# Half-size products of an attention and feed-forward kernel: transposes moved right behind the scores, both lumps of products at the tile's end, results taken out one tile later

## The chip, the core and the metric

The kernel runs on one core of a Trainium2 chip. The metric is the device time of one execution in microseconds (us). The engines are named as in the profile: PE (TensorE matmul) with its weight loads PEld, DVE (VectorE), ACT (ScalarE), POOL (GpSimd), and SP, which issues the DMAs here.

## The reference

The first half is attention with a threshold: of each row of scores only those within `tau` of the row's maximum count. The second half is two matrix products with an activation between them.

```python
scores = scale * np.matmul(q, k.transpose(0, 1, 3, 2))        # 8 batches, 8 heads, 576 x 64
thresh = np.max(scores, axis=-1, keepdims=True) - tau
scores = np.where(scores >= thresh, scores, -1000000000.0)
attn = np.exp(scores - np.max(scores, axis=-1, keepdims=True))
attn = attn / (np.sum(attn, axis=-1, keepdims=True) + 1e-09)
x = np.matmul(attn, v)                                        # then to (4608, 512)
h = x @ w_in                                                  # 512 -> 2048
g = h * np.tanh(np.log1p(np.exp(np.minimum(h, 20.0))))        # h itself above 20
out = g @ w_out                                               # 2048 -> 512
```

## The kernel before

**Attention** runs over 32 head pairs (8 batches of four), each in nine tiles of 128 rows, so `NT` is 288. One pass of the loop at line 764 is the step `g`; `g % 9` is called the position of its tile here. The instructions of each engine keep the order in which the code issues them (class `InOrder`, line 60), so the order of calls in a step is the order on the engines. All their rows carry line 70, that of the helper; they are told apart by tile names.

In step `g`, PE makes the scores `s` of tile `g + 1` (`begin`), four matmuls, or eight for the tile of position 8. DVE takes the row maximum of tile `g` and two small scalings (`st`), ACT makes the exponential `e`, and DVE masks and sums it into `p` (`masked`). In the next step POOL scales `p` (`normalise`). In the step after that PE transposes it into PSUM (`transposes`): four blocks into `tp`, and in odd tiles and position 8 a fifth into `t` (`t5` in the code). One step later ACT copies them to `hi`, `lo` and `tk` (`evacuate`). Twice in a pair, in the steps of positions 8 and 4, PE multiplies them with the values into `y` (`values`), ten matmuls; ACT takes `y` out into `x` in the following step. `y` and `t` share one PSUM bank.

**The first product** `h = x @ w_in` is fed into the same loop, as a generator `stream` from which `advance(stream, n)` takes `n` matmuls. For batches 2 to 5 (`SEVEN`), in steps 117 to 260 (`FROM` to `TO`, in the code `seven`), `gemm1_seven` works with seven half-size products where eight would be needed. For each of eight `j` it makes the products named in `steps` (line 681), each of six matmuls of 288 columns. They use three accumulators `a`, `b`, `c` in PSUM that take turns in two banks (`psh`, tag `ph`), so a product needs the bank of the last but one before it, and that one's result has to be taken out first. A result leaves PSUM in one of two ways: ACT copies it to `hst` (`copy`; for two of the four copies POOL then adds the first result, from the list `sides`), or DVE adds it to what is in `hst` (`add`; the last one also issues the store of `hst` to DRAM and, a step later, the load of the weight sums `wt` three `j` ahead).

A tile has two products, except at positions 4 and 8, where `y` is made (`EVEN` is 0 there): seven tiles with fourteen products a pair, two `j`. The first product of a tile (a lump of six matmuls) stands right behind the scores, the transposes behind it, the second lump at the end of the step. When a product ends, the generator puts the taking out of its result into the list `leaves`. Those of the second lump are carried over to the next step (`waiting`): copies in front of the exponential, adds behind the reciprocal. Those of the first lump are issued in the same step, behind the exponential. At positions 0 and 5 `evacuate` stands behind the exponential, otherwise in front of everything that ACT does in the step.

Behind these come, in each step, the gathering of `y` (`done`), and the `chores`: splitting `q`, `k` and `x` into a high and a low part (a cast on ACT, a subtraction on POOL: `q`, `k`, `xh`, `xl`), and at the end of a batch the differences of `x` (subtractions on DVE, `parts_x`, and their splits, `parts_t`).

Of the kernel before, what the change touches and what calls it, by code (L numbers as in the profile page):

```python
# [135 lines left out]
def attention_moe(tc, q, k, v, tau, w_in, w_out, out):  # L136
# [3 lines left out]
    with ExitStack() as outer:  # L140
# [108 lines left out]
        with ExitStack() as first:  # L249
# [6 lines left out]
            with ExitStack() as att:  # L256
# [369 lines left out]
                def gemm1_seven(b, made):  # L626
# [27 lines left out]
                    def run(j):  # L654
# [17 lines left out]
                        def add(name, other, last=False):  # L672
# [9 lines left out]
                            ("a", "A", "b11", 0, nc.scalar, copy, "21"),  # L682
                            ("b", "1", "t2", 0, nc.scalar, copy, "12", True),
                            ("a", "B", "b21", 1, nc.scalar, copy, "11"),
                            ("b", "2", "t3", 0, nc.scalar, copy, "22", True),
                            ("c", "0", "t1", 0, nc.vector, add, "22", "22"),
                            ("b", "C", "t4", 1, nc.vector, add, "21", "21"),
                            ("c", "3", "b22", 1, nc.vector, add, "12", "12", True),
                        )
                        for bank, w, x, end, engine, kind, *names in steps:  # L690
                            for h in product(j, bank, w, x, end):
                                if h is not None:
                                    leaves.append((engine is nc.scalar, lambda h=h, kind=kind, names=names: kind(*names)(h)))
                                yield
# [43 lines left out]
                def leave_tile(g):  # L738
                    evacuate(g % 9, *tiles[g]["tp"], pairs[g // 9]["pt"])
                    del tiles[g]  # L740
# [23 lines left out]
                for g in range(NT + 6):  # L764
# [16 lines left out]
                    if seven and EVEN[g % 9]:  # L781
                        advance(stream, 6)
# [4 lines left out]
                    if 3 <= g < NT + 3:  # L787
                        if not (seven and g % 9 in (0, 5)):
                            leave_tile(g - 3)
                    for scalar, work in waiting:  # L790
                        if scalar:
                            work()
                    if ahead:
                        tiles[g - 2]["tp"] = transposes(g - 2)
                    done = ready
                    ready = []
                    for _ in range(5 if g >= SOON else PIECES):
                        if pieces:
                            work, then = pieces.pop(0)
                            work()  # L800
                            if then:
                                (done if g >= NT else ready).append(then)
# [6 lines left out]
                    if seven and g % 9 in (0, 5):  # L809
                        leave_tile(g - 3)  # L810
# [8 lines left out]
                    for scalar, work in [m for m in waiting if not m[0]] + leaves:  # L819
                        work()  # L820
                    leaves.clear()
                    while sides:
                        sides.pop(0)()
                    for gather, closed in done:
                        gather()
                        if closed is not None:
                            close_pair(g, closed)
                    for work in chores.pop(g, []):
                        work()
# [31 lines left out]
                    if not seven:  # L861
                        advance(stream, DRAIN if g >= NT else (SLOW if 78 <= g < FROM else EVEN)[g % 9])
                    if g < len(WARM[1]):
                        warm_up(WARM[1][g])
                    if not ahead and 2 <= g < NT + 2:
                        tiles[g - 2]["tp"] = transposes(g - 2)
                    if seven and EVEN[g % 9]:
                        advance(stream, 6)
# [185 lines left out]
```

## Time and profile before

| | us |
|---|---|
| three runs | 1356.60, 1356.62, 1355.78 |
| median | 1356.6 |
| the profiled execution, its own time | 1356.75 |
| its span | 1355.0 |
| stretch with half-size products (first to last matmul that reads `wt`) | 365 to 829 |

| busy, whole span | us | share |
|---|---|---|
| PE | 1295.1 | 96% |
| weight loads | 1144.3 | 84% |
| DVE | 953.6 | 70% |
| ACT | 864.3 | 64% |
| POOL | 828.4 | 61% |

A row of the profile's timeline has the start in us from the span's start, the duration, the engine, the line, the operation with output and inputs, and a count of merged instructions; in brackets how long the engine had been idle and what ended that. Matmuls are pipelined: the step from one start to the next tells what one costs, and their durations overlap. A row of the waits has the engine and tile that waited, what for, the total in us, the count and the longest.

### The profile page before, as it was taken

Reading aid. Unit: us, or ns where it says so; the run is one execution under the profiler, and the core shown is the slowest. Engines: PE = TensorE matmul, PEld = TensorE weight load, DVE = VectorE, ACT = ScalarE, POOL = GpSimd, SP = SyncE. Lnnn points to the kernel's source line nnn. Section 1 sums busy time; section 2 is a strip of 40 time slices with the busy share of each in tenths; the row PEclk is TensorE's granted clock in tenths of the full one; section 3 lists DMA queues with packets and bytes.
Section 4 is the critical chain, followed back from the end, with each engine's and each line's share of the span. In section 5 each row is a group of like instructions: output and inputs, shape, how many; then the busy total and the mean of one; then the engine's idle time right before and its main releaser. Section 6 shows DMA issues by size and latency. Waiting matters only on the chain. (4 is left out here: it accounts for less than half of the span.)

```text
span 1355.0 us, 28749 instructions
## 1 busy us (share of the span) xinstructions
PE 1295.1 (96%) x9749; PEld 1144.3 (84%) x9749; DVE 953.6 (70%) x2564; ACT 864.3 (64%) x1716; POOL 828.4 (61%) x1165
## 2 busy tenths in 40 slices
PE   8787999999999999999999999999999999999998
PEld 5445899898878878877887888989979999999998
DVE  6998887777766766676676666563986666666664
ACT  4786887777766666676666666664656555555552
POOL 3788897777876786787678677642403334444331
PEclk9987999999999999999999999999999999999999
DMA  5444455767456546545645655313745443444440
GB/s 175 119 128 129 142 163 149 221 201 228 142 173 195 153 151 186 166 148 179 189 152 158 188 161 170 99 42 100 249 150 156 125 140 110 140 141 137 138 131 32
DMA packets 174434, 205.17 MB, mean 151 GB/s; under 512 B 29392, under 2 KB 147152, under 8 KB 170192
## 3 DMA queue, kind: packets, MB, share of 16 engines
q1 hardware_dynamic: 174288, 203.34, 49.5%
q8 instruction: 77, 1.26, 0.4%
q14 instruction: 69, 0.57, 0.1%
HBM read 143.52 MB, written 59.77 MB: 150 GB/s over the span
## 5 line engine op out<-in xcount | busy, mean ns | idle before, releaser
L70 DVE SCALAR_TENSOR_TENSOR p<-s,st,e 128x576 f32<-128x576 f32 x288 | 234.8, 815 | 204.6 <-ACT e L70 204.3
L70 POOL TENSOR_SCALAR p<-p,st 128x576 f32<-128x576 f32 x288 | 246.1, 854 | 92.9 <-DVE st L70 37.5
L70 ACT ACTIVATE e<-s,st 128x576 f32<-128x576 f32 x288 | 216.3, 751 | 133.1 <-DVE st L70 129.2
L70 PE MATMUL s<-k,q 128*128 128x288 f32 (+1 forms) x1280 | 237.7, 331 | 31.0 <-DVE p L70 28.5
L70 POOL TENSOR_TENSOR z<-z 128x256 f32<-128x256 f32 x128 | 124.4, 976 | 223.0 <-DVE z L70 214.2
L70 PEld LDWEIGHTS s<-k,q 128*128 128x128 f32 (+1 forms) x1280 | 172.5, 190 | 57.0 <-DVE p L70 51.8
L70 DVE TENSOR_REDUCE st<-s 128x1 f32<-128x576 f32 x288 | 216.7, 753 | 2.7 <-PE s L70 2.7
L70 DVE TENSOR_TENSOR gl<-z,gh 128x1792 fp32r<-128x1792 f32 (+1 forms) x72 | 141.7, 1969 | 108.1 <-ACT gh L70 108.1
L70 PE MATMUL h<-xh,w1h 128*128 128x288 f32 x704 | 212.4, 302 | 2.6 <-DVE hst L70 2.0
L70 ACT CAST gh<-z 128x1792 fp32r<-128x1792 f32 (+1 forms) x72 | 116.6, 1621 | 149.7 <-issue 81.1
L70 PE MATMUL h<-xl,w1h 128*128 128x288 f32 x704 | 208.9, 297 | 0.7 <-POOL xl L70 0.7
L70 PE MATMUL h<-xh,w1l 128*128 128x288 f32 x704 | 208.1, 296 | 0.0
L70 PE MATMUL tp<-ident,p 128*128 128x128 f32 x1152 | 179.8, 279 | 4.5 <-POOL p L70 2.8
L70 PEld LDWEIGHTS tp<-ident,p 128*128 128x128 f32 x1152 | 134.3, 141 | 45.1 <-issue 16.4
L70 PE MATMUL o<-gh,sl 128*128 128x256 f32 x512 | 144.5, 282 | 0.0
L70 PE MATMUL o<-gl,sh 128*128 128x256 f32 x512 | 143.8, 281 | 0.0
L70 PE MATMUL o<-gh,sh 128*128 128x256 f32 x512 | 143.5, 280 | 0.0
L70 PE MATMUL y<-hi,vf 128*64 128x320 f32 (+1 forms) x512 | 141.4, 417 | 0.4 <-ACT tk L70 0.4
L70 PE MATMUL y<-lo,vf 128*64 128x320 f32 (+1 forms) x512 | 141.4, 417 | 0.0
L70 PEld LDWEIGHTS h<-xh,w1h 128*128 128x128 f32 x704 | 133.9, 190 | 4.5 <-DVE hst L70 2.9
L70 PE MATMUL o<-gl,w2h 128*128 128x256 f32 (+1 forms) x448 | 133.3, 298 | 1.3 <-DVE gl L70 1.3
L70 PE MATMUL o<-gh,w2h 128*128 128x256 f32 (+1 forms) x448 | 133.3, 298 | 1.3 <-DVE hst L70 1.3
(77 smaller groups left out, 3209.5 us busy)
## 6 DMA issues: line engine op xcount, KB each, us to landing
z<-hd SPq DMA_DIRECT2D x144, 256.0 KB, 3.1
wt<-sw SPq DMA_DIRECT2D x32, 1024.0 KB, 6.3
r<-q SPq DMA_DIRECT2D x112, 160.0 KB, 2.5
r<-k SPq DMA_DIRECT2D x112, 160.0 KB, 2.3
hd<-hst SPq DMA_DIRECT2D x56, 256.0 KB, 6.2
vf<-v SPq DMA_DIRECT2D x64, 160.0 KB, 3.8
out_t<-c SPq DMA_DIRECT2D x36, 256.0 KB, 2.4
dec<-w_in SPq DMA_DIRECT2D x32, 256.0 KB, 3.7
```

The source lines that it names most:

```text
L70: made = method(*args, **kwargs)
```

## The change

Only the stretch of batches 2 to 5 is touched. The transposes of a tile move up to stand right behind the scores, and the matmuls of `y` stand behind them. Both lumps are taken from the stream at the step's end, twelve matmuls in one go. All results are carried over to the next step, where copies and adds are issued behind the exponential, `normalise` and the gathering of `y`, in the order of the products. `evacuate` stands in front of the exponential in all positions. The core of the diff (left out: the engine's name goes from the rows of `steps`; `multiply` is the old loop over `pieces` under a name):

```diff
-                        for bank, w, x, end, engine, kind, *names in steps:
+                        for bank, w, x, end, kind, *names in steps:
...
-                                    leaves.append((engine is nc.scalar, lambda h=h, kind=kind, names=names: kind(*names)(h)))
+                                    leaves.append(lambda h=h, kind=kind, names=names: kind(*names)(h))
...
                     waiting, leaves[:] = leaves[:], []
-                    if seven and EVEN[g % 9]:
-                        advance(stream, 6)
...
                     if 3 <= g < NT + 3:
-                        if not (seven and g % 9 in (0, 5)):
-                            leave_tile(g - 3)
-                    for scalar, work in waiting:
-                        if scalar:
-                            work()
+                        evacuate((g - 3) % 9, *tiles[g - 3]["tp"], pairs[(g - 3) // 9]["pt"])
+                        del tiles[g - 3]
...
-                    for _ in range(5 if g >= SOON else PIECES):
-                        if pieces:
-                            work, then = pieces.pop(0)
-                            work()
-                            if then:
-                                (done if g >= NT else ready).append(then)
+                    if not seven:
+                        multiply(5 if g >= SOON else PIECES)
...
                         exponential(tiles[g]["s"], tiles[g]["st"], tiles[g]["e"])
-                    if seven and g % 9 in (0, 5):
-                        leave_tile(g - 3)
...
-                    for scalar, work in [m for m in waiting if not m[0]] + leaves:
-                        work()
-                    leaves.clear()
-                    while sides:
-                        sides.pop(0)()
                     for gather, closed in done:
                         gather()
                         if closed is not None:
                             close_pair(g, closed)
+                    for work in waiting:
+                        work()
+                    for work in sides:
+                        work()
+                    sides.clear()
+                    if seven:
+                        tiles[g - 2]["tp"] = transposes(g - 2)
+                        multiply(5)
...
-                    if not seven:
+                    if seven:
+                        advance(stream, 12 if EVEN[g % 9] else 0)
+                    else:
                         advance(stream, DRAIN if g >= NT else (SLOW if 78 <= g < FROM else EVEN)[g % 9])
...
-                    if not ahead and 2 <= g < NT + 2:
+                    if not ahead and not seven and 2 <= g < NT + 2:
                         tiles[g - 2]["tp"] = transposes(g - 2)
-                    if seven and EVEN[g % 9]:
-                        advance(stream, 6)
```

PE, the tile of position 3 in the first pair of the stretch, before (`tp` and `t_` are the transposes, `h` the products, those from `w1h` and `w1l` being the first product of the next `j`):

```order
L70 MATMUL s<-k_4902,q_4901 128x288
L70 MATMUL s<-k_4903,q_4901 128x288
L70 MATMUL h<-xh,wt 128x288
L70 MATMUL h<-xl,wt 128x288
L70 MATMUL h<-xh,wt 128x288 x2
L70 MATMUL h<-xl,wt 128x288
L70 MATMUL h<-xh,wt 128x288
L70 MATMUL tp<-ident,p 128x128 x4
L70 MATMUL t_5618<-ident,p 128x128
L70 MATMUL h<-xh,w1h 128x288
L70 MATMUL h<-xl,w1h 128x288
L70 MATMUL h<-xh,w1l 128x288
```

And the same place of the change:

```order
L70 MATMUL s<-k_4902,q_4901 128x288
L70 MATMUL s<-k_4903,q_4901 128x288
L70 MATMUL tp<-ident,p 128x128 x4
L70 MATMUL t_5600<-ident,p 128x128
L70 MATMUL h<-xh,wt 128x288
L70 MATMUL h<-xl,wt 128x288
L70 MATMUL h<-xh,wt 128x288 x2
L70 MATMUL h<-xl,wt 128x288
L70 MATMUL h<-xh,wt 128x288
L70 MATMUL h<-xh,w1h 128x288
L70 MATMUL h<-xl,w1h 128x288
L70 MATMUL h<-xh,w1l 128x288
```

The five transposes changed places with the first lump of six.

ACT, positions 0 and 1 of a pair, before (`h_7592` and `h_7631` are the two banks of the products, `tp_` and `t5_` the transposes, `y_7551` the values' result):

```order
L70 ACTIVATE e_7600<-s_7546,st_7599 128x576
L70 COPY hi1_7503<-tp_7582 128x4x128
L70 COPY hst_7609<-h_7592 128x288
L70 COPY x_7611<-y_7551 128x256
L70 CAST q0_7520<-r_7527 128x320
L70 CAST q0_7520<-r_7529 128x320
L70 COPY tk1_7505<-t5_7629 128x128
L70 COPY lo1_7504<-tp_7624 128x4x128
L70 COPY hst_7609<-h_7631 128x288
L70 ACTIVATE e_7653<-s_7587,st_7652 128x576
L70 COPY hst_7609<-h_7592 128x288
L70 CAST q1_7523<-r_7577 128x320
```

And of the change:

```order
L70 COPY hi1_7495<-tp_7567 128x4x128
L70 ACTIVATE e_7594<-s_7545,st_7593 128x576
L70 COPY x_7602<-y_7550 128x256
L70 CAST q0_7520<-r_7527 128x320
L70 CAST q0_7520<-r_7529 128x320
L70 COPY tk1_7497<-t5_7609 128x128
L70 COPY lo1_7496<-tp_7604 128x4x128
L70 ACTIVATE e_7644<-s_7587,st_7643 128x576
L70 COPY hst_7652<-h_7622 128x288
L70 COPY hst_7652<-h_7629 128x288
L70 CAST q1_7523<-r_7582 128x320
```

The copy of `tp` stands in front of the first exponential instead of behind it, `x` right behind it, and both product copies stand behind the second exponential.

More of the change, by code (lines that the diff above doesn't have):

```diff
@@ L681, in run @@
                         steps = (
[L682 to L688, printed above, removed]
+                            ("a", "A", "b11", 0, copy, "21"),
+                            ("b", "1", "t2", 0, copy, "12", True),
+                            ("a", "B", "b21", 1, copy, "11"),
+                            ("b", "2", "t3", 0, copy, "22", True),
+                            ("c", "0", "t1", 0, add, "22", "22"),
+                            ("b", "C", "t4", 1, add, "21", "21"),
+                            ("c", "3", "b22", 1, add, "12", "12", True),
                         )
-                        for bank, w, x, end, engine, kind, *names in steps:
+                        for bank, w, x, end, kind, *names in steps:
                             for h in product(j, bank, w, x, end):
                                 if h is not None:
-                                    leaves.append((engine is nc.scalar, lambda h=h, kind=kind, names=names: kind(*names)(h)))
+                                    leaves.append(lambda h=h, kind=kind, names=names: kind(*names)(h))
                                 yield
@@ L736, in product, with multiply @@
                         pieces.append((some[-1], (gather, pi if t == 8 else None)))
-                def leave_tile(g):
-                    evacuate(g % 9, *tiles[g]["tp"], pairs[g // 9]["pt"])
-                    del tiles[g]
+                def multiply(n):
+                    for _ in range(n):
+                        if pieces:
+                            work, then = pieces.pop(0)
+                            work()
+                            if then:
+                                ready.append(then)
                 def close_pair(g, pi):
@@ L787, in attention_moe @@
                     if 3 <= g < NT + 3:
-                        if not (seven and g % 9 in (0, 5)):
-                            leave_tile(g - 3)
-                    for scalar, work in waiting:
-                        if scalar:
-                            work()
+                        evacuate((g - 3) % 9, *tiles[g - 3]["tp"], pairs[(g - 3) // 9]["pt"])
+                        del tiles[g - 3]
                     if ahead:
                         tiles[g - 2]["tp"] = transposes(g - 2)
-                    done = ready
-                    ready = []
-                    for _ in range(5 if g >= SOON else PIECES):
-                        if pieces:
-                            work, then = pieces.pop(0)
-                            work()
-                            if then:
-                                (done if g >= NT else ready).append(then)
+                    done, ready[:] = ready[:], []
+                    if not seven:
+                        multiply(5 if g >= SOON else PIECES)
+                    if g >= NT:
+                        done += ready
+                        ready.clear()
                     if g < NT:
@@ L827, in attention_moe @@
                             close_pair(g, closed)
+                    for work in waiting:
+                        work()
+                    for work in sides:
+                        work()
+                    sides.clear()
+                    if seven:
+                        tiles[g - 2]["tp"] = transposes(g - 2)
+                        multiply(5)
                     for work in chores.pop(g, []):
```

## The prediction

> **What bounds the kernel now.** I read the page first, then the busy time of the stretch that the edit touches, then its waits, then its timeline engine by engine. "Position" below is a tile's place 0 to 8 in its head pair. The profiled execution took 1356.75 us, 1355.0 of them the span:
>
> ```profile
> span 1355.0 us, 28749 instructions
> 365.00:829.00 464.00, 440.07 (x3257) 376.21 (x3258) 314.67 (x1112) 310.63 (x735) 348.60 (x528) 1.00 0.55 167
> ```
>
> The second row is the stretch with half-size products, 365 to 829 us (they are the matmuls that read wt). Its columns are length, then busy time of PE, weight loads, DVE, ACT and POOL, then the granted clock. PE is busy for 440 of 464 us at full clock, and the others for 311 to 349, so PE sets the pace, and what the edit can win is PE's own waiting. These are the waits of that stretch (total us, times, longest):
>
> ```profile
> DVE p L70 <- ACT e L70: 106.1, 91, 2.7
> PEld t L70 <- ACT x L70: 19.4, 32, 0.6
> ACT hst L70 <- PE h L70: 18.3, 44, 0.7
> PEld s L70 <- DVE p L70: 18.2, 48, 1.6
> PEld h L70 <- DVE hst L70: 2.9, 4, 0.7
> PEld tp L70 <- POOL p L70: 2.3, 4, 0.6
> PEld h L70 <- POOL xl L70: 1.6, 4, 0.4
> ```
>
> PE's side has three kinds. It waits 32 times for the copy x<-y before a fifth transpose t, 48 times for the mask p before scores s, and 12 times in small amounts where a batch ends. DVE's 106 us are waits for the exponential e, and the ACT row says why e can be late: ACT stands waiting for PE's h in front of it.
>
> PE's timeline shows their size. Rows are start, duration, operation, count:
>
> ```profile
> 501.32 0.69 PE L70 MATMUL s<-k,q 128*128 128x288 f32 x4
> 502.64 0.60 PE L70 MATMUL tp<-ident,p 128*128 128x128 f32 x4
> 503.00 0.38 PE L70 MATMUL h<-xh,wt 128*128 128x288 f32 x1
> 503.87 1.22 PE L70 MATMUL s<-k,q 128*128 128x288 f32 x8
> 505.73 0.60 PE L70 MATMUL tp<-ident,p 128*128 128x128 f32 x4
> 506.17 0.27 PE L70 MATMUL t<-ident,p 128*128 128x128 f32 x1
> 507.18 0.79 PE L70 MATMUL s<-k,q 128*128 128x288 f32 x4
> 509.68 0.60 PE L70 MATMUL y<-tk,vf 128*64 128x256 f32 x4
> 510.21 0.66 PE L70 MATMUL tp<-ident,p 128*128 128x128 f32 x4
> 510.62 0.77 PE L70 MATMUL s<-k,q 128*128 128x288 f32 x4
> 512.03 0.61 PE L70 MATMUL tp<-ident,p 128*128 128x128 f32 x4
> 513.00 0.33 PE L70 MATMUL t<-ident,p 128*128 128x128 f32 x1 [0.36 <-ACT x L70]
> 532.33 1.22 PE L70 MATMUL s<-k,q 128*128 128x288 f32 x8
> ```
>
> The two x8 rows are position 7 of neighbouring pairs: a pair takes 28.46 us. Position 6 runs without a wait in 2.55 us (501.32 to 503.87); its four scores and first six h take 1.32 (501.32 to 502.64), 0.132 each, so four scores are 0.53 and six h 0.79. A free fifth transpose follows its four after 0.44 us (505.73 to 506.17); at position 0 it follows after 0.97 (512.03 to 513.00), so one such wait costs 0.53 us. The other side of it, ACT and DVE at the same moment:
>
> ```profile
> 508.85 0.82 DVE L70 SCALAR_TENSOR_TENSOR p<-s,st,e 128x576 f32<-128x576 f32 x1 [0.32 <-ACT e L70]
> 510.65 0.74 ACT L70 ACTIVATE e<-s,st 128x576 f32<-128x576 f32 x1 [1.83 <-DVE st L70]
> 511.29 0.58 ACT L70 COPY hi<-tp 128x512 f32<-128x512 f32 x1
> 511.43 0.82 DVE L70 SCALAR_TENSOR_TENSOR p<-s,st,e 128x576 f32<-128x576 f32 x1 [0.70 <-ACT e L70]
> 512.27 0.40 ACT L70 COPY hst<-h 128x288 f32<-128x288 f32 x1 [0.40 <-issue]
> 512.57 0.38 ACT L70 COPY x<-y 128x256 f32<-128x256 f32 x1
> ```
>
> ACT does e, then hi, then a product copy hst for which it waits, and only then x. The two mask rows give DVE's own loop, mask to mask through row maximum and e: 2.58 us (1.80 to the start of e, 0.78 from there).
>
> **What PE loses in all.** The weight-load rows overstate a wait a little: 19.4/32 is 0.61 where the matmuls lose 0.53, so I take 0.08 off each. For x: 32 x 0.53 = 17.0 us. For the mask: 18.2 - 48 x 0.08 = 14.4. For the 12 at batch ends: 6.8 - 12 x 0.08 = 5.8. Together 37.2 us, the most that removing waits can bring.
>
> **Part by part.** *Same work.* No instruction is added or removed: 12 product matmuls in each of seven tiles of nine, the same copies, adds and DMAs. Only waits and changes of operand kind can move. The latter the rows bound: four transposes take 0.36 us when h follows (502.64 to 503.00) and 0.41 when scores follow (510.21 to 510.62). I take nothing, and keep 144 tiles x 0.05 = 7 us either way for the range.
>
> *x copied right behind e (positions 0 and 5, each after a value tile).* The value tile keeps its 3.44 us (507.18 to 510.62), now with transposes ahead of y. y's last row ends at 510.28, 0.07 us after the next work on PE started. The new fifth transpose is due after four scores and four transposes, 0.53 + 0.44 = 0.97 us into the next tile. If e is done, x takes 0.38 from 0.07 on and is there at 0.45. If DVE gains no lead, e still begins 3.47 us after the value tile's scores (510.65 - 507.18), x follows at 4.11 and ends at 4.49, where the transpose is due at 3.44 + 0.97 = 4.41: a wait of about 0.1. So between 13 and 17 of the 17.0 us go; I take 15.
>
> *Product copies behind e.* ACT no longer waits for PE's h in front of e, since the copies belong to the tile before and stand behind e. That frees DVE to run at 2.58 us while PE needs 2.55 to 3.98 a tile, and the waits for the mask go. What keeps them are tiles where DVE itself is longer, at the end of a batch:
>
> ```profile
> 474.09 0.82 DVE L70 TENSOR_TENSOR hst<-h,hst 128x288 f32<-128x288 f32 x2 [0.84 <-POOL hst L70]
> 474.83 1.46 DVE L70 TENSOR_TENSOR x<-x 128x288 f32<-128x288 f32 x2
> 475.43 0.29 PE L70 MATMUL h<-xh,wt 128*128 128x288 f32 x1
> 476.21 0.81 DVE L70 SCALAR_TENSOR_TENSOR p<-s,st,e 128x576 f32<-128x576 f32 x1
> 477.08 0.79 PE L70 MATMUL s<-k,q 128*128 128x288 f32 x4 [1.35 <-DVE p L70]
> ...
> 713.03 0.79 PE L70 MATMUL s<-k,q 128*128 128x288 f32 x4 [1.37 <-DVE p L70]
> ```
>
> Here two subtractions (1.46 us) stand in front of the mask, and scores start 1.65 us after the last h instead of 0.13. The row at 713.03 is the last of three such places, with the same idle time. Three times 1.52 are 4.6 us; I keep half of it. 14.4 - 2.3 = 12.1. Of the 5.8 us at batch ends I take half, 2.9, since POOL's chain there starts from the earlier x, but the transposes also ask for p earlier. Sum of the gains: 30.0.
>
> *The new wait.* Both lumps now stand at the tile's end, and each needs its PSUM bank emptied by a copy or add of the tile before, queued behind e (of this tile). From a mask's start M the first copy ends at M + 1.80 + 0.64 + 0.40 = M + 2.84. PE's scores can start at the earliest 0.87 after the mask's start (476.21 to 477.08), and the lump 0.53 + 0.36 later: M + 1.76. So in lockstep PE would wait 1.08 us; it waits for nothing once DVE leads by as much. DVE gets that lead in the value tile (3.44 against 2.58: 0.86 us; more in the other, wider one) and at position 7 with its eight scores (3.31 against 2.58), and keeps it as long as ACT keeps up. ACT's fullest tile is this one, e to e with a copy on either side, a cast and the four pieces of tile 8:
>
> ```profile
> 514.48 0.79 ACT L70 ACTIVATE e<-s,st 128x576 f32<-128x576 f32 x1
> 515.49 0.40 ACT L70 COPY hst<-h 128x288 f32<-128x288 f32 x1 [0.22 <-PE h L70]
> 517.44 0.75 ACT L70 ACTIVATE e<-s,st 128x576 f32<-128x576 f32 x1
> ```
>
> 2.96 - 0.22 of waiting = 2.74 us against PE's 2.55: 0.19 of lead lost per pair. At position 7 an add now waits for a copy behind the same e (both products of one lump): the copy ends 1.04 after e's start, the add takes 0.41 (474.09, two in 0.82), so the mask comes 1.45 after e's start and not 0.78, 0.67 later, against PE's 0.73 of extra scores. I charge 3 us in all (16 pairs x 0.19).
>
> The Trainium skill's page "TensorE: Matmul & The Clock Gate" (Part 4) gives a 128x128 transpose inside a kernel about 275 ns; if that were the step from one to the next, four would hold the lump off by 1.1 us and a lead of about 0.3 would do, an estimate from that page, which would take the 3 us out of the sum. The trace shows 0.27 only as duration; the step is 0.36/4 = 0.09 us, and I go by that.
>
> *SP and POOL.* The stores from hst and the loads of wt move a tile later on SP, past loads of r. A store lands in 8.3 us at most, and its buffer is needed again two groups later, a group being half a pair, 14.2 us: covered, with some 6 us to spare. POOL's p must be ready 0.79 us earlier (six h fewer in front of the transposes):
>
> ```profile
> DMA to landing us min/median/max: 1.6/4.7/8.3
> 518.52 0.83 POOL L70 TENSOR_SCALAR p<-p,st 128x576 f32<-128x576 f32 x1
> 519.57 0.80 PE L70 MATMUL s<-k,q 128*128 128x288 f32 x4
> ```
>
> p is done at 519.35, and the transposes would follow the scores at 519.57 + 0.53: 0.75 us to spare, in one of the tighter tiles.
>
> **Sum.** 15 + 12.1 + 2.9 - 3 = 27.0 us. The profiled run would take 1356.75 - 27.0 = 1329.75; the median of the runs, 1356.6, lies 0.15 lower, so I forecast 1329.6.
>
> **Rivals.** *Half of it goes to bank waits.* The lead of DVE is used up twice a pair, after each value tile's gain, and PE pays half of 1.08 us each time: 32 x 0.54 = 17 us, gain 10, 1346.6. For it: ACT's 2.74 us. Against it: the value tiles renew the lead, and PE's own wait renews it too.
>
> *The products wait every time: slower.* Place: lumps of positions 1, 2, 6 and 7, whose first product needs an ACT copy. If ACT, with its copies behind e and its casts behind those, takes longer from e to e than PE's 2.55 to 2.8 us, no lead stands, and each pays 1.08: 64 x 1.08 = 69 us against 30 gained, 1396. It decides from 0.47 us a lump on. For it: the fullest tile's 2.74 us. Against it: ACT is busy 311 of 464 us. The page "PSUM — Partial Sum Buffer" of the Trainium skill (Summary: rules for kernel authors) says to evacuate promptly, which is this rival's rule; here PE waited for hst at only four places (2.9 us), so the trace before neither bears it out nor refutes it.
>
> *The wait moves to the transposes.* If POOL's adds, behind the later copies, delay p past the 0.75 us, five tiles a pair could pay some 0.32 each, the longest wait that the row of POOL xl shows, 0.4, less 0.08: 16 x 5 x 0.32 = 26 us, and next to nothing is gained, 1355.6. Against it: POOL's 349 of 464 us.
>
> **Chances and range.** Forecast 0.60, half of it 0.18, no gain 0.09, products waiting 0.13. A measurement of this kernel can tell about 0.2%, 2.7 us. Faster by more: 0.60 + 0.18 = 0.78. Within: 0.07 of the third rival. Slower: 0.13 + 0.02 = 0.15. The range goes from all waits and the operand changes won, 1356.6 - 37.2 - 7 = 1312.4 (I say 1313), to the first rival with 3 us more, 1350; it leaves out the other two rivals, 0.22.
>
> **What would show it.** Right: the waits of t for x fall from 32 x 0.6 to a few us; DVE's wait for e shrinks; ACT's wait for h in front of hst is gone; an ordinary pair takes about 27.0 us from x8 to x8. Wrong: new rows of h waiting for ACT hst or DVE hst at 64 or more places, or of tp waiting for POOL p; a pair at 28.4 us or more.

## The result, and the profile after

| | before | changed |
|---|---|---|
| median on one chip, us | 1356.19 | 1325.68 |
| its runs, us | 1353.98 to 1356.62 | 1324.67 to 1328.44 |
| profiled execution, its own time, us | 1356.75 | 1325.35 |
| ratio of the times | | 0.9781, 95% interval 0.9763 to 0.98 |

The gain is 31.4 us between the two profiled executions and 30.5 between the medians, where 27.0 were forecast. All ratios here and below are against runs of the kernel before that were taken beside those of the kernel named. The page and the busy time of the stretch with half-size products, which now ends at 797 us (columns as before: length, then busy time of PE, weight loads, DVE, ACT, POOL, then the granted clock):

```profile
span 1323.6 us, 28739 instructions
365.00:797.00 432.00, 423.70 (x3251) 375.68 (x3251) 322.87 (x1117) 310.97 (x734) 347.30 (x527) 1.00 0.59 179
```

The span is 31.4 us shorter and the stretch some 31 (365 to 829 before, 365 to 797 now), so all of the gain lies there. ACT and POOL are as busy as they were (311 and 347 us): no work went, only waiting. Some rows of the waits of this stretch (total us, times, longest):

```profile
DVE p L70 <- ACT e L70: 62.1, 90, 1.1
...
PEld s L70 <- DVE p L70: 8.1, 12, 1.2
PEld tp L70 <- POOL p L70: 5.2, 8, 1.1
...
DVE hst L70 <- PE h L70: 2.7, 11, 0.3
```

The row of `t` waiting for `x` (19.4 us, 32 times) is gone from the list, that of scores waiting for the mask fell from 48 to 12 times, and no `h` waits for ACT's `hst`. The last row is one that I had not read before; in the kernel before it is

```profile
DVE hst L70 <- PE h L70: 17.6, 26, 1.1
```

so DVE no longer stands waiting for PE's products. Rows of PE's timeline over one ordinary pair, from one `x8` to the next:

```profile
521.27 1.23 PE L70 MATMUL s<-k,q 128*128 128x288 f32 x8
...
527.85 0.79 PE L70 MATMUL s<-k,q 128*128 128x288 f32 x4
528.48 0.60 PE L70 MATMUL tp<-ident,p 128*128 128x128 f32 x4
528.91 0.27 PE L70 MATMUL t<-ident,p 128*128 128x128 f32 x1
...
531.70 0.38 PE L70 MATMUL h<-xh,w1h 128*128 128x288 f32 x1
...
534.26 0.38 PE L70 MATMUL h<-xh,wt 128*128 128x288 f32 x1
...
547.85 1.23 PE L70 MATMUL s<-k,q 128*128 128x288 f32 x8
```

A pair takes 26.58 us (521.27 to 547.85), before 28.46. The steps from scores to scores, by position, in this pair and in that of before from 503.87 us (here and below they are the distances of such rows):

| position | 7 | 8 | 0 | 1 | 2 | 3 | 4 | 5 | 6 | pair |
|---|---|---|---|---|---|---|---|---|---|---|
| before | 3.31 | 3.44 | 3.34 | 2.79 | 2.82 | 2.88 | 3.99 | 3.33 | 2.56 | 28.46 |
| changed | 3.21 | 3.37 | 2.75 | 2.77 | 2.58 | 2.67 | 3.90 | 2.77 | 2.56 | 26.58 |

Positions 0 and 5 lost 0.59 and 0.56 us (the waits for `x`), 2, 3 and 7 together 0.55 (the waits for the mask), 4 and 8 0.09 and 0.07 (the value tiles; the account of the prediction below comes back to them). At 528.91 the fifth transpose follows its four after 0.43 us: it waits for nothing. ACT at the same moment:

```profile
527.96 0.37 ACT L70 COPY x<-y 128x256 f32<-128x256 f32 x1 [0.40 <-PE y L70]
529.86 0.76 ACT L70 ACTIVATE e<-s,st 128x576 f32<-128x576 f32 x1
530.50 0.71 ACT L70 COPY hst<-h 128x288 f32<-128x288 f32 x2
...
533.41 0.69 ACT L70 COPY hst<-h 128x288 f32<-128x288 f32 x2
```

`x` is ready at 528.33, 0.48 us into the tile and 0.58 ahead of its transpose. The copies of the products end their first half about 0.40 after they start, at 530.90 and 533.81, and the lumps that need the bank begin at 531.70 and 534.26: 0.8 and 0.45 us to spare. The second is the tightest place of the pair.

What is left stands at the batch ends, where a pair takes 30.07 us (464.63 to 494.70) and not 26.55:

```profile
466.31 1.88 DVE L70 TENSOR_TENSOR x<-x 128x288 f32<-128x288 f32 x2
468.98 0.80 PE L70 MATMUL s<-k,q 128*128 128x288 f32 x4 [0.99 <-DVE p L70]
482.54 0.66 PE L70 MATMUL tp<-ident,p 128*128 128x128 f32 x4 [0.81 <-POOL p L70]
483.27 0.82 DVE L70 TENSOR_TENSOR hst<-h,hst 128x288 f32<-128x288 f32 x2 [2.36 <-POOL hst L70]
483.79 0.40 PE L70 MATMUL h<-xh,wt 128*128 128x288 f32 x1 [0.48 <-DVE hst L70]
```

Two subtractions again stand in front of the mask at position 7, and at position 3 PE waits for POOL's `p` and, through DVE, for POOL's `hst`.

### The profile page after: what moved, and what is told of

Same layout as the page of the kernel before. It is cut to its first block, busy times and chain, and to the rows that moved or that the text cites. A ratio compares the mean times of both kernels' runs of the same rounds, so it can differ in the third digit from the quotient of the medians.

```text
span 1323.6 us, 28739 instructions
## 1 busy us (share of the span) xinstructions
PE 1281.0 (97%) x9749; PEld 1144.4 (86%) x9749; DVE 963.7 (73%) x2564; ACT 865.5 (65%) x1716; POOL 827.7 (63%) x1165
## 5 line engine op out<-in xcount | busy, mean ns | idle before, releaser
L70 PE MATMUL s<-k,q 128*128 128x288 f32 (+1 forms) x1280 | 234.0, 328 | 23.3 <-DVE p L70 22.2
L70 PEld LDWEIGHTS tp<-ident,p 128*128 128x128 f32 x1152 | 136.9, 141 | 34.9 <-POOL p L70 10.3
L70 ACT COPY hi<-tp 128x512 f32<-128x512 f32 (+1 forms) x160 | 87.5, 547 | 90.2 <-PE tp L70 88.4
```

Of the source, the lines that this page charges most:

```text
L70: made = method(*args, **kwargs)
```

## The experiments

Theory A is the prediction's: copies out of the way of `x` win some 17 us, and product copies behind the exponential take ACT's wait for `h` away from it, so that DVE gets a lead and the mask is in time. The rivals are that the transposes count by themselves, that both lumps and late results lead to bank waits, and, later, theory M (below): that adds on DVE hold the mask up. The first eight runs test the parts.

### Product copies behind the exponential, alone

The kernel before, with the carried copies behind the exponential:

```diff
-                    for scalar, work in waiting:
-                        if scalar:
-                            work()
...
-                    for scalar, work in [m for m in waiting if not m[0]] + leaves:
+                    for scalar, work in waiting + leaves:
```

> The kernel before, with one thing of the change: the product copies that were carried over stand behind the exponential instead of in front of it. The orders on PE and the evacuations stay as before. Theory A (the waits of PE go because ACT is free in front of the exponential, and because x is copied right behind it, and these are two separate gains): the waits of scores for the mask fall from 18.2 us to under 8, the 32 waits of the fifth transpose for x stay at about 17 us or a little less; an ordinary pair falls from 28.45 to 27.8-28.2 us, the time to 1343-1350. Theory B (what counts is the order on PE, transposes next to the scores and twelve products in one go): nothing moves, 1354-1358.

Measured: 1356.17 us, ratio 1.0 (0.999 to 1.001). The two kinds of wait stay as they were, and so does ACT's wait for `h`:

```profile
PEld t L70 <- ACT x L70: 18.8, 31, 0.6
PEld s L70 <- DVE p L70: 18.5, 48, 1.7
ACT hst L70 <- PE h L70: 17.7, 41, 0.7
```

A's second half predicted that the second row would go. It did not. The third row says why: the copies that wait for `h` in the kernel before are those of the first lump, which stood behind the exponential already. In the rows that the prediction shows, the copies at 512.27 and 515.49 us wait 0.40 and 0.22 us, each behind an exponential; the carried copy, in front of the exponential of 514.48, starts without a wait:

```profile
514.19 0.43 ACT L70 COPY hst<-h 128x288 f32<-128x288 f32 x1
```

### Product copies in front again

The changed kernel, with the carried copies back in front of the exponential:

```diff
+                    for scalar, work in waiting:
+                        if scalar:
+                            work()
...
-                    for work in waiting:
-                        work()
+                    for scalar, work in waiting:
+                        if not scalar:
+                            work()
```

> The changed kernel, with the product copies in front of the exponential again, right behind the evacuation. The order on PE stays that of the change. Theory A: ACT again waits for products of PE in front of the exponential, the mask comes late and scores wait for it: an ordinary pair rises from 26.55 to 27-28 us, the time from 1325.7 to 1332-1348. Theory B: no change, 1324-1328. Theory C (the banks bind: copies behind the exponential come almost too late for the lump): earlier copies help, under 1324.

Measured: 1325.71 us, ratio 0.9776 (0.9761 to 0.979), the pair 26.61 us. ACT waits for PE as long in all as in the kernel before, and here it does so in front of the exponential:

```profile
ACT hst L70 <- PE h L70: 18.9, 43, 1.2
```

and yet the row of scores waiting for the mask is gone. So the place of the copies is worth nothing by itself in either kernel, and a wait of ACT for `h` in front of the exponential does not make the mask late.

### The transposes back between the lumps

The changed kernel, PE's order in a product tile as before:

```diff
-                    if seven:
+                    if seven and not EVEN[g % 9]:
                         tiles[g - 2]["tp"] = transposes(g - 2)
...
-                        advance(stream, 12 if EVEN[g % 9] else 0)
+                        if EVEN[g % 9]:
+                            advance(stream, 6)
+                            tiles[g - 2]["tp"] = transposes(g - 2)
+                            advance(stream, 6)
```

> The changed kernel, with the transposes of a tile with products back between the two lumps (scores, six products, transposes, six products), the rest as in the change. Theory A: the fifth transpose is due 0.8 us later, so x is there in time all the more, and the mask is not touched; but the first lump is due 0.4 us earlier after the copies that empty its bank, and ACT gets the transposes 0.8 us later, in front of the exponential. A pair of 26.5 to 27.2 us, time 1325-1336. Theory B (the order on PE is the gain): the 0.5 us a pair that no named wait explains come back, and more: a pair of 27.1 us and above, 1334 or more, with no new waits in the trace.

Measured: 1355.39 us, ratio 0.9993 (0.9983 to 1.0002): the whole gain is gone. The waits for `x` and for the mask are all but gone as well; a new one has taken their place, 48 times. Its row, and PE and ACT over two tiles:

```profile
PEld h L70 <- ACT hst L70: 36.1, 48, 1.6
```

```profile
512.14 0.40 PE L70 MATMUL h<-xh,w1h 128*128 128x288 f32 x1 [0.46 <-ACT hst L70]
...
513.68 0.38 ACT L70 COPY hi<-tp 128x256 f32<-128x256 f32 x1 [0.93 <-PE tp L70]
514.67 0.74 ACT L70 ACTIVATE e<-s,st 128x576 f32<-128x576 f32 x1
515.31 0.69 ACT L70 COPY hst<-h 128x288 f32<-128x288 f32 x2
515.75 0.40 PE L70 MATMUL h<-xh,wt 128*128 128x288 f32 x1 [0.57 <-ACT hst L70]
```

This is a loop, a ring of instructions in which each waits for the one before it: the first lump, the transposes behind it, their copies on ACT, the exponential behind those, the product copies behind that, and only then the bank for the next first lump: 3.61 us from 512.14 to 515.75, where a tile of PE's work takes 2.55. Positions 1, 2 and 6 step by 3.49, 3.40 and 3.28 us. It is the second rival of the prediction, and its condition (ACT longer from one exponential to the next than PE) is met here because ACT itself waits 0.93 us for `tp`. In the changed kernel the transposes stand in front of the lump, and the loop is cut.

### The evacuation behind the exponential at positions 0 and 5

The changed kernel with the exception of the kernel before kept:

```diff
-                        evacuate((g - 3) % 9, *tiles[g - 3]["tp"], pairs[(g - 3) // 9]["pt"])
-                        del tiles[g - 3]
+                        if not (seven and g % 9 in (0, 5)):
+                            leave_tile(g - 3)
...
+                    if seven and g % 9 in (0, 5):
+                        leave_tile(g - 3)
```

> The changed kernel, with the copy of tp behind the exponential again in the tiles of positions 0 and 5 (as in the kernel before), so in front of the copy of x. Theory A: x comes 0.58 us later where ACT is busy until then, but in the change x is ready some 0.4 us before the fifth transpose is due if DVE leads: between 0 and 0.3 us for 32 tiles, 1325-1335. Were the place of this copy what held x up before, the wait would come back in full: 0.53 x 32 = 17 us, 1343.

Measured: ratio 0.9789 (0.9773 to 0.9805), the profiled execution 1327.95 us against 1325.35, ordinary pairs 26.57. By the intervals that is not to be told from nothing. The steps show a small loss all the same: the pairs ahead of the batch ends take 26.92 to 26.97 us instead of 26.55, those at the batch ends 30.3 instead of 30.1, some 2 us in all.

### Product copies made twice

The changed kernel with each of ACT's product copies issued twice, so that the bank comes free later:

```diff
+                                nc.scalar.copy(to[name], h)
                                 nc.scalar.copy(to[name], h)
```

> The changed kernel, with each of the 128 product copies on ACT done twice over (0.30 us each more, same values). Theory A2: in the change the first copy is done 0.8 us before its lump at position 1 and 0.45 us before it at position 2; twice 0.30 us in the tile of position 1 and one more at position 2 use that up: waits of h for hst of some 0.2 to 0.6 us at one or two positions a pair, 5 to 20 us in all, 1330-1345. If ACT had ample room: no change, 1324-1328. If ACT were the bound already: all of 128 x 0.30 = 38 us, 1360 and more.

Measured: 1334.71 us, ratio 0.9838 (0.9823 to 0.9853), the pair 27.14 us.

```profile
PEld h L70 <- ACT hst L70: 15.5, 26, 1.2
```

Position 2, the one with 0.45 us to spare, goes from 2.58 to 3.15 us. The bank waits are near, and the tightest place read from the timeline is the one that gives first.

### The subtractions first at the batch ends

The changed kernel, with the differences of `x` ahead of the product adds on DVE:

```diff
-                        later(at + (n // 2 if k else n), add, *names)
+                        firsts.setdefault(at + (n // 2 if k else n), []).append(lambda names=names: add(*names))
...
+                    for work in firsts.pop(g, []):
+                        work()
```

> The changed kernel, with the subtractions of x at a batch's end in front of the product adds on DVE instead of behind them. Theory A2: what is left of the waits for the mask are three places where two subtractions (1.5 us) stand behind an add that waits for its copy behind the exponential; in front of it they fill that wait. The three waits of 1.16 us go, or most of them: 1322-1325, 2 to 3.5 us under the change. If the subtractions are what is long, wherever they stand: no difference.

Measured: 1325.48 us, ratio 0.9765 (0.9752 to 0.9779): no change. The wait at position 7 went (its step is 3.20 us), but positions 0 and 2 grew to 3.40 and 3.47, and the pair is 30.15. The wait moved: what comes last there is not set by DVE's order alone.

### `x` first

The kernel before, with the gathering of `y` in front of the products' copies of the same tile, and nothing else:

```diff
+                    for gather, closed in done:
+                        gather()
+                        if closed is not None:
+                            close_pair(g, closed)
                     for scalar, work in [m for m in waiting if not m[0]] + leaves:
                         work()
                     leaves.clear()
...
-                    for gather, closed in done:
-                        gather()
-                        if closed is not None:
-                            close_pair(g, closed)
```

> The kernel before, with one thing of the change: the copy of y into x stands in front of the product results that are taken out in the same step, no longer behind them. Orders on PE and everything else as before. Theory A2 (one chain: at positions 0 and 5 x stands behind a product copy that waits for the first lump of the same tile, the fifth transpose waits for x, ACT waits for the transpose, and the next exponentials come late; the waits of scores for the mask are the tail of it): the 32 waits of the fifth transpose fall from 17 us to under 4, the waits for the mask fall too, an ordinary pair goes from 28.45 to 26.9-27.4 us, the time to 1328-1342. Rival D (x is only one of several things that hold ACT up, the product copy then stands where x stood, and the tail stays): a pair of 27.4-28.4 us, 1343-1356.

Measured: 1339.99 us, ratio 0.9875 (0.9862 to 0.9889). The waits for `x` are gone and the mask's are not, against theory A2, which had them as one chain:

```profile
PEld s L70 <- DVE p L70: 19.2, 51, 1.6
```

A pair takes 27.27 us. So 16.5 us, over half of the gain, come from the order of four lines. The rest needs something else.

### Transposes between the lumps, copies in front

The third experiment's kernel, transposes between the lumps and results a tile later, with its product copies in front of the exponential (the diff is that of the second experiment).

> The changed kernel with the transposes back between the two lumps (as in the experiment that lost the whole gain), and in addition the product copies in front of the exponential. Theory A2: what cost that experiment 36 us is a loop: first lump, transposes, their copy on ACT, exponential, product copy, first lump of the next tile, 0.79 + 0.44 + 0.15 + 0.59 + 0.64 + 0.40 = 3.0 us and latencies, where PE needs 2.6. With the copy in front of the exponential the 0.64 drops out, the loop is about 2.4-2.7 us, and the waits of h for hst fall from 36 us to under 10: 1326-1336, so that the place of the transposes is free again. Rival: the lump waits since it comes 0.4 us earlier, whatever stands in between: the waits stay over 20 us, 1345 or more.

Measured: 1343.01 us, ratio 0.9896 (0.9882 to 0.9911).

```profile
PEld h L70 <- DVE hst L70: 18.0, 16, 2.6
PEld h L70 <- ACT hst L70: 4.7, 16, 0.9
```

The waits for ACT's copies fall from 36.1 to 4.7 us: the exponential was a link of that loop, as read. A wait for DVE's add at position 3 (its step 3.34 instead of 2.67 us) comes up in its place, so the time is above the 1336 us expected and the kernel still isn't faster than `x` first alone.

### Theory M: the adds in front of the mask

What the eight runs leave is the mask. Theory M reads it off DVE: an add of the tile's *first* product stands in front of the mask and waits for PE. DVE of the kernel before, position 7 (the scores that follow start at 507.18, quoted in the prediction):

```profile
505.93 0.46 DVE L70 TENSOR_TENSOR hst<-h,hst 128x288 f32<-128x288 f32 x1 [1.04 <-PE h L70]
506.31 0.81 DVE L70 SCALAR_TENSOR_TENSOR p<-s,st,e 128x576 f32<-128x576 f32 x1
```

Scores, first product, add, mask, next scores: the chain starts from PE in the same tile, so DVE can never be ahead of PE by more than this chain allows. With results a tile later the add's data are there already. It is tested from two sides. First, `x` first, with those adds behind the mask:

```diff
-                    for scalar, work in [m for m in waiting if not m[0]] + leaves:
+                    behind = [work for scalar, work in leaves if not scalar]
+                    for scalar, work in [m for m in waiting if not m[0]] + [m for m in leaves if m[0]]:
...
                         tiles[g]["p"] = masked(g, tiles[g]["s"], tiles[g]["st"], tiles[g]["e"], half)
+                    for work in behind:
+                        work()
```

> This is the kernel before with x<-y copied right behind the exponential (the earlier run e9_x_first, 1339.99 us, pair 27.27 us, 50 waits of scores for the mask of 19.0 us in all) and one thing more: DVE's adds of the tile's first product stand behind the mask instead of in front of it. Theory M: what makes the mask late in the kernel before is that DVE stands waiting for a product of the same tile (an add in front of the mask, idle for h), so that DVE can have no lead. Then the waits of scores for the mask fall from 19.0 us to under 9 us, an ordinary pair from 27.27 to 26.7 to 27.0 us, and the time to 1329 to 1336 us. Rival: the mask is late for the exponential alone, whose chain starts from the scores; then the waits stay at 17 to 20 us, the pair at 27.2 to 27.4 and the time at 1338 to 1342 us. A second rival: an add behind the mask gives its bank up later, and the next product waits for it (new rows of h waiting for DVE hst of 10 us or more); then the time is 1338 us or more though the waits for the mask are gone.

Measured: 1356.59 us, ratio 1.0001 (0.9992 to 1.001).

```profile
PEld h L70 <- DVE hst L70: 25.0, 19, 2.6
PEld s L70 <- DVE p L70: 8.9, 22, 1.0
```

```profile
522.55 0.46 DVE L70 TENSOR_TENSOR hst<-h,hst 128x288 f32<-128x288 f32 x1 [1.36 <-POOL hst L70]
523.07 0.40 PE L70 MATMUL h<-xh,wt 128*128 128x288 f32 x1 [0.92 <-DVE hst L70]
```

The second rival of the expectation took the time: at position 3 the add, which now comes late and here waits 1.36 us for POOL's sum first, holds its bank, and the step goes from 2.87 to 4.15 us. But the mask's waits fell by 10.3 us, and positions 2 and 7 step by 2.56 and 3.22 us where they had 2.83 and 3.31, which are the changed kernel's 2.58 and 3.21. There M holds.

Second, `x` first with the transposes alone moved, so that they lie inside M's chain:

```diff
-                    if seven and EVEN[g % 9]:
-                        advance(stream, 6)
...
+                    if seven:
+                        tiles[g - 2]["tp"] = transposes(g - 2)
+                    if seven and EVEN[g % 9]:
+                        advance(stream, 6)
                     for scalar, work in [m for m in waiting if not m[0]] + leaves:
```

> The kernel before with x<-y copied right behind the exponential (the earlier run e9_x_first, 1339.99 us, pair 27.27 us) and only the transposes of the change: they stand right behind the scores, the first product behind them; every result leaves PSUM when it did before, so the adds of the first product still stand in the same tile, in front of the mask. With the earlier runs this closes a square: neither (e9_x_first, 1340.0), results a tile later alone (e3_tr_between, 1355.4), both (the changed kernel, 1325.7), transposes alone (this one). Theory M: at positions 2, 3 and 7 a loop sets the pace, scores, first product, DVE's add, mask, next scores but one, and the transposes put into it lengthen it by their 0.36 to 0.44 us. Then these three steps, in e9_x_first 2.82, 2.87 and 3.31 us, grow by 0.25 to 0.45 us each, the waits of scores for the mask rise from 19 to 30 to 40 us, an ordinary pair takes 28.0 to 28.7 us, and the time is 1351 to 1363 us. Rival: the transposes' place counts by itself and the mask is late only for the exponential; then the pair is 26.6 to 27.4 us and the time 1326 to 1342 us.

Measured: 1408.72 us, ratio 1.0384 (1.0366 to 1.0401), pairs of 32.0 us. The sign is M's, the size is well over what I expected. Waits (365 to 870 us), and position 7:

```profile
PEld s L70 <- DVE p L70: 40.2, 47, 1.7
DVE hst L70 <- PE h L70: 32.0, 32, 2.3
PEld tp L70 <- POOL p L70: 20.7, 34, 0.8
```

```profile
518.53 1.23 PE L70 MATMUL s<-k,q 128*128 128x288 f32 x8
521.14 0.46 DVE L70 TENSOR_TENSOR hst<-h,hst 128x288 f32<-128x288 f32 x1 [1.25 <-PE h L70]
521.52 0.81 DVE L70 SCALAR_TENSOR_TENSOR p<-s,st,e 128x576 f32<-128x576 f32 x1
522.39 0.79 PE L70 MATMUL s<-k,q 128*128 128x288 f32 x4 [0.49 <-DVE p L70]
```

The chain of M is there link by link: from scores to the add's start 2.61 us (before 505.93 - 503.87 = 2.06), mask 0.38 later, scores 0.87 after that. Against `x` first, positions 7 and 3 grow by 0.55 and 0.56 us, a little over the 0.25 to 0.45 expected. But that is 1.1 of the 4.7 us by which a pair grows. Position 2 grows by 0.83, and positions 0, 1, 5 and 6, which are not in M's chain, by 0.79, 0.82, 0.45 and 0.75.

There the transposes come late. The third row puts that down to POOL's `p`, but the `p` that they read had long been done. PE, ACT and POOL from position 0 to 1:

```profile
526.11 0.82 POOL L70 TENSOR_SCALAR p<-p,st 128x576 f32<-128x576 f32 x1 [0.92 <-PE tp L70]
527.22 0.63 PE L70 MATMUL tp<-ident,p 128*128 128x128 f32 x4 [0.61 <-ACT hi L70]
528.84 0.40 ACT L70 COPY hst<-h 128x288 f32<-128x288 f32 x1 [1.49 <-issue]
530.01 0.60 ACT L70 COPY lo<-tp 128x512 f32<-128x512 f32 x1
530.71 0.63 PE L70 MATMUL tp<-ident,p 128*128 128x128 f32 x4 [0.63 <-POOL q L70]
```

The transposes at 530.71 read the `p` that POOL scaled by 526.93, 3.8 us earlier. What ended just before them, at 530.61, is the copy of the last tile's `tp`, and they need it, since the kernel has one buffer for `tp` (pool `pst`, `bufs=1`). On ACT that copy stands behind the copy of the first product, which waits for the first lump, which on PE now stands behind the transposes: a second loop, 3.49 us from 527.22 to 530.71, where a tile of PE's work takes 2.55. In nearly all pairs of the stretch the transposes of positions 1, 2 and 6 start 0.10 us after a copy of `tp` has ended; at 0 and 5 they start 0.14 us after the copy that this kernel keeps behind the exponential. So the mask's loop has 1.1 to 1.9 of the 4.7 us, by whether position 2 is counted to it, and the waits for the one `tp` buffer have the rest. That is read from the trace; no run took the two apart.

### The square

These runs with the changed kernel make a square (all with `x` ahead of the product results of its step; medians in us):

| | results out as before | results a tile later |
|---|---|---|
| transposes between the lumps | 1340.0 | 1355.4 |
| transposes behind the scores | 1408.7 | 1325.7 |

Either part alone loses, 15.4 and 68.7 us; both together win 14.3. The two on the right also have the product copies behind the exponential and evacuate in front of it everywhere. The second is worth some 2 us in the changed kernel. With the product copies in front, as on the left, the right column reads 1343.0 and 1325.7: late results alone then lose only 3.0, and both together win as much.

### POOL relieved at the batch ends

The changed kernel, with the low halves of one difference (`t4`) made on DVE one step later, and then with three low halves there and the subtractions first. The core of both:

```diff
+                def halve_apart(step, home, n, to, at, x):
+                    to[at] = [home.tile([P, HB], F32R, name=f"x{m}", bufs=n) for m in "hl"]
+                    xh, xl = to[at]
+                    nc.scalar.copy(xh, x)
+                    firsts.setdefault(step, []).append(lambda: nc.vector.tensor_tensor(xl, x, fv(xh), ALU.subtract))
```

> The changed kernel, with the low halves of the last batch-end difference (two subtractions of 128x288 for each of four batches) made on DVE a step later instead of on POOL. Theory B: the pairs at the batch ends (30.1 us against 26.55 of an ordinary one) are bound by POOL's chain, which is busy without a gap there and late with p and with hst. Then these four pairs take 28.2 to 29.3 us, and the time falls by 3 to 8 us to 1317.5 to 1322.5 us. Rival: DVE, which gets the work, is as late as POOL was, since it has the differences of x to make at the same place; then the pairs stay at 29.8 us or more and the time within 1323.5 to 1328 us.

> The changed kernel, with both: the differences of x ahead of the product adds on DVE at the batch end (alone in e6_subs_first: no change), and three of the low halves taken from POOL to DVE a step later. Theory B: with POOL relieved the order on DVE counts too; the four pairs at the batch ends take 27.8 to 28.8 us and the time is 1315.5 to 1320.5 us. Rival: DVE is now the one that is late; pairs of 29.8 us or more and 1323.5 us or more.

Measured: 1321.79 us, ratio 0.9749 (0.9734 to 0.9763), pairs of 28.97 us at the batch ends; and 1319.68 us, ratio 0.973 (0.9717 to 0.9744), pairs of 28.4 to 28.7. In the first the wait of `tp` for POOL's `p` at position 3 is gone (its step 3.38 instead of 4.43 us), in the second that of the scores at position 7 as well. So POOL was the bound at position 3; the pairs are still some 2 us longer than an ordinary one. With POOL relieved, the order on DVE, which alone had done nothing, and one more half brought 2 us together; how much of it is each was not tested. The second is the fastest version found, 2.7% below the kernel before and 0.5% below the changed one.

## Why the prediction was right, and where it was wrong

- *Sum and place.* Forecast 27.0 us of gain, measured 31.4. Fifteen pairs of the stretch can be laid side by side, from the `x8` at 385.92 us before and 385.01 now. Nine ordinary ones lose 1.90 each, three at a batch end 1.51, the three ahead of those 2.93 (29.48 to 26.55): 17.1 + 4.5 + 8.8 = 30.4 us. By position, 0 and 5 lose 17.2 of them, 2, 3 and 7 lose 11.1, the value tiles 4 and 8 lose 2.1.
- *`x`: right.* Taken 15 of 17.0. `x` first alone brought 16.5, and over the fifteen pairs it is the 17.2 of positions 0 and 5. The computed moment (ready 0.45 us into the tile, due at 0.97) is there in the trace: 0.48 and 1.06.
- *Mask: the size about right, the reason wrong.* The step that failed is "ACT no longer waits for PE's h in front of e ... That frees DVE". Moving those copies did nothing in either kernel (ratio 1.0, and 0.9776 against 0.9781), and in the kernel before the copies that wait stand behind the exponential. I had taken the row of DVE waiting for `e` and ACT's row beside it as one chain, and not looked at DVE's own rows in front of the mask. What went is the add that waited for a product of the same tile. This is shown at positions 2 and 7; at 3 it is argued from the changed kernel's step alone, since the run meant to show it put a bank wait there. That the sum came near with this reason in it is luck in part: the rows of the waits told how much there was to win, not what would win it, and the change happened to move the adds as well.
- *Mask and batch ends together: a little too much.* 15.0 us taken, 11.1 + 2.1 = 13.2 measured with the value tiles (next point). The prediction counted three places where subtractions stand in front of the mask. The steps before show six: position 7 takes 4.31 to 4.35 us in the pairs ahead of the batch ends too. Those three are gone (3.20 us, 3.4 us in all). At the ends POOL's chain kept its wait, and position 3 even grew by some 0.27 each.
- *Operand kinds: taken at nothing, and nothing is shown.* The value tiles became 0.16 us a pair shorter. But with the adds behind the mask and the transposes in their old place position 8 takes 3.34 us as well: there `y` follows its scores after 0.62 us (510.03 to 510.65), and after 0.72 where the scores had waited (507.18 to 507.90). So at position 8 it is the tail of the mask's wait; for position 4 that is argued.
- *The new wait: charged 3 us, cost nothing.* No `h` waited for ACT. But the lead is thin, 0.45 us at position 2, and the doubled copies show it.
- *The rivals.* None came to pass in the change. The second, the products' wait, is the kernel with late results alone. The third, the transposes' wait for POOL's `p`, shows in the change only where a batch ends (5.2 us in all, 0.81 at the position 3 quoted); early transposes alone lose to loops that no rival of the prediction named. The prediction took the gains as parts that add up. They don't: the waits are loops, and each part cuts the loop that the other would close. Early transposes cut the one from the first lump over the transposes' copy and the exponential to the product copy; late results cut the two that go through the results of the first product.
- *Evacuating at once.* Early transposes with results out in the same tile, 1408.7 us, against results a tile later, 1325.7: here the later one wins by 83 us (the changed kernel also evacuates the transposes earlier at two positions, which is worth some 2). The Trainium skill's page "PSUM — Partial Sum Buffer" (Summary: rules for kernel authors) says to evacuate promptly; it gives the tightness of the memory as its reason, and the run with late results alone (1355.4 against 1340.0) goes its way. What decided between them was the loop on which the emptying instruction stood.

## What to carry to other kernels

Where several engines hand a tile round, write down each loop with its links (who waits for whom, and what stands in front of it in that engine's queue) and compare its length with the pace of the bound engine; a change of order is judged by the loops it closes or cuts, not by a sum over the waits that it removes. Don't take the engine that a row of waits names for the cause before its time of ending fits: in one of the runs here POOL was named where ACT's copy came last. An instruction that takes in a result of the same step costs most in front of the one that the bound engine waits for: carrying results over one step is free only if the bank they hold isn't asked for first. And try the halves of a change apart: here the cheapest one, four lines, held over half of the gain.

## What was not expected of the hardware

The same subtraction on DVE, both inputs in SBUF, takes between 0.44 and 0.96 us in the changed kernel. Two of them, and what POOL did beside them:

```profile
444.28 0.44 DVE L70 TENSOR_TENSOR x<-x 128x288 f32<-128x288 f32 x1
444.54 0.88 POOL L70 TENSOR_SCALAR p<-p,st 128x576 f32<-128x576 f32 x1 [0.92 <-DVE st L70]
445.77 1.71 POOL L70 TENSOR_TENSOR q<-r,q 64x320 fp32r<-64x320 f32 x2 [0.35 <-ACT q L70]
446.84 0.96 DVE L70 TENSOR_TENSOR x<-x 128x288 f32<-128x288 f32 x1
```

POOL was idle until 444.54, for over half of the first, and scaled `p` during the rest; during most of the second it was in the middle of its own subtractions. The Trainium skill's page "SBUF — State Buffer" (Who interferes with whom) says that a DVE instruction with two SBUF inputs contends with a GpSimd instruction that reads SBUF; the two rows agree. It would also explain why the pair of subtractions at the batch end (466.31, 1.88 us) came out longer than the 1.46 us from which the prediction worked; no run took POOL's work away beside them to show it.
